# Attention and MLP on one core: the inner layer's upper part in one step for 18 groups, and the first block products' operands in the plan

## The chip, the cores and the metric

The kernel runs on one core of one Trainium2 chip. The metric is the device time of an execution in microseconds (us). Three runs of the kernel before took 776.96, 771.91 and 774.73 us, a median of 774.73; a fourth execution was profiled.

## The reference

Block-sparse attention is followed by a two-layer network (cut; inputs are 4 batches, 8 heads, 768 positions of 64; the network has 3072 tokens, 512 wide, and an inner width of 2048). `w_in` and `w_out` come as 64-bit floats, the rest of the large inputs as 32-bit.

```python
def _attn_ref(q, k, v, sampled_blocks):
    scores = scale * np.matmul(q, k.transpose(0, 1, 3, 2))
    # blocks of 32: neighbours, first and last block, 3 sampled blocks per row
    scores = np.where(mask, scores, -1000000000.0)
    scores = scores - np.max(scores, axis=-1, keepdims=True)
    attn = np.exp(scores)
    attn = attn / (np.sum(attn, axis=-1, keepdims=True) + 1e-09)
    return np.matmul(attn, v).astype(np.float32)

def _moe_ref(x, w_in, w_out, s, b):
    h = x @ w_in
    r = np.maximum(h, 0.0)
    g = s * (r * r) + b
    return (g @ w_out).astype(np.float32)
```

## The kernel before

**Stages.** Attention fills the first 250 us. The network follows in two stages. In the first, tokens 0 to 767 (two groups of 384 tokens) go through the network in 32 *groups*: a group is 384 tokens by 128 of the inner width. In the second, the other 2304 tokens go through it as products of blocks by Strassen's scheme: the inner width is taken in eight passes of two blocks of 128, and each pass needs seven block products instead of eight.

**Accuracy.** A 32-bit product is made of three matmuls. Every operand is split into an upper part (rounded to the type `fp32r` by a copy) and a lower part (operand less upper part): `upper*upper + upper*lower + lower*upper`. So each operand costs a cast on ScalarE (ACT) and a subtraction on VectorE (DVE).

**One group.** `mlp1` makes the first matrix of a group on TensorE (PE), 12 matmuls of 384 columns into bank 0 or 1 by turns (L438 to L440). Then come `relu` (L443, ACT), `square` (L448 on ACT for groups from `SQ` = 24 on, else L450 on DVE, which also multiplies by `s`), `hidden_high` (L454 adds `b`, L455 casts, both on ACT) and `hidden_low` (L459, DVE). `mlp2` makes the second matrix of the group before, nine matmuls of 512 columns (L480 to L482). The tiles are called `hid0` and `hid1` for the working tiles, `hid2` to `hid4` for upper parts and `hid5` to `hid7` for lower ones.

**Weights.** A 64-bit block is loaded by SyncE (SP) into a raw buffer (L62) and decoded into the two parts in nine steps of `decode_f64`: on DVE L85 and L87, L93, L94, L95; on POOL L88; on ACT the sign (L89) and two Relus with a bias (L91, L92). The biases are the tiles `b_top` and `b_most`, filled by POOL at the start. There are 32 blocks, `i0` to `i15` and `o0` to `o15`. Six are decoded during attention, the others beside the groups, and `o15` is the last.

**What sets the order.** An object of class `Plan` collects attention, the decoding and the first `NPL` = 30 groups as operations with an engine, a cost, a priority, dependencies and buffers, and works out an order for every engine; the instructions are then issued in that order, and each engine takes its own strictly one after the other. The costs are written into the code, as in the tuple `cost` of the decoding. Groups 30 and 31 and all block products are issued behind the plan, by loops written out. Which sums and splits stand beside which product is in tables: `EARLY` (behind groups 30 and 31), `FIRST` (behind the products of the first pass), `F_NOW`, `F_NEXT` and so on. A word such as `+S2` is a sum (L575 of weights, L577 and L580 of `x`), `wA21` joins two parts of a weight quarter (L584), `<B11` is a load (SP), `>A21` a store, `hS2` and `lS2` are the upper part (L599, ACT) and the lower part (L601, DVE).

**The first block products.** `product` (L605 to L618) takes two operands, one of weights (A, S) and one of `x` (B, T), and makes six matmuls of 384 columns in bank 0 or 1 by turns (the same two banks as the groups). The order is 1, 2, 6, 7, 5, 3, 4. The plan holds some of the operands already, placed behind the last raw load by `last_load`: loads and splits of B11 and B21, the sums S1, S2, S3, T3, T1, T2, and the two parts of S2. Product 1 is copied by ACT (L1461) and the others are added to it by DVE (L1465 and on). The part before the first product reads:

```python
    EARLY = {30: "hT3 lT3 hS3 lS3", 31: "<B22 hT2 lT2 hT1 hS1"}
    for i in range(NPL, NSUB):
        g, f = subs[i]
        mlp1(i)
        relu(i)
        if i - LAG >= NPL - 1:
            mlp2(i - LAG)
        square(i)
        hidden_high(i)
        hidden_low(i)
        work(0, S0, EARLY.get(i, ""))
```

## Time and profile before

| | |
|---|---|
| median of three runs | 774.73 us |
| profiled execution | 772.34 us |
| its span | 770.6 us |
| mean granted TensorE clock | 0.986 of full speed |
| TensorE busy | 732.4 us |
| DVE busy | 568.1 us |
| ACT busy | 475.1 us |
| POOL busy | 242.1 us |
| moved by DMA | 89.14 MB |

How to read the lines of the profile: a group of instructions is a line of the kernel, engine, operation, tile written and tiles read, partitions by elements, and a count; then the busy time in us, the mean of one in ns, the idle time of the engine just before them and what ended it. A line of the timeline is the start in us from the span's beginning, the duration, the engine, the line, the operation, the tiles, and, in brackets, the idle time ahead and what released it. A line of the stretches is the stretch, its length, the busy time and instruction count of PE, PEld (weight loads of TensorE), DVE, ACT and POOL, the granted clock, the busy share of the DMA engines and GB/s. A line of SP's waits is what the queue waited at and for, then the sum in us, the count and the longest.

### The profile page before, as it was taken

What the parts mean: (1) busy time and instruction counts of PE and PEld (TensorE: products, weight loads), DVE (VectorE), ACT (ScalarE), POOL (GpSimd) and SP (SyncE); (2) the same over time, 40 slices, a digit from 0 to 9 for tenths busy, and PEclk for the clock granted to TensorE, in tenths of its full rate; (3) what the DMA queues carried; (4) which work ended last, traced back from release to release, by engine and by line L of the source; (5) the groups of instructions that cost most, each with busy time, mean ns of one, the idle gap of its engine ahead of it and who ended that gap; (6) DMA issues with size and microseconds to landing.
All of it is one profiled execution on the core that took longest, in us unless ns stands there. A gap on an engine that the chain in (4) does not pass through costs nothing.

```text
span 770.6 us, 21377 instructions
## 1 busy us (share of the span) xinstructions
PE 732.4 (95%) x8032; PEld 619.7 (80%) x8032; DVE 568.1 (74%) x1437; ACT 475.1 (62%) x1143; POOL 242.1 (31%) x398
## 2 busy tenths in 40 slices
PE   8699898999788999999989999999999999999997
PEld 6377675676567999999878998888998998888896
DVE  4767466988586789897896688687678678667652
ACT  3767576888586878789753444565443567344433
POOL 4936244546230221211022232223222232222221
PEclk9989999999899999999999999999999999999999
DMA  8978888877774534635433222224000022000002
GB/s 237 235 199 223 233 215 223 206 202 213 178 202 117 159 110 148 209 118 161 101 126 90 76 83 75 63 69 123 1 1 1 1 62 83 1 1 0 1 1 82
DMA packets 100998, 89.14 MB, mean 116 GB/s; under 512 B 50208, under 2 KB 79520, under 8 KB 100896
## 3 DMA queue, kind: packets, MB, share of 16 engines
q1 hardware_dynamic: 98592, 81.50, 37.8%
q0 software_dynamic: 2304, 6.29, 3.3%
q8 instruction: 63, 1.03, 0.6%
q14 instruction: 39, 0.32, 0.1%
HBM read 68.89 MB, written 14.68 MB: 108 GB/s over the span
## 4 chain that ended last, share of the span: by engine, by line
PE 75%; DVE 9%; ACT 5%; issue 4%; DMA 3%; POOL 1%; SPq 1%; POOLq 0%; ACTq 0%; DVEq 0%
PE m L617 20%; PE o L481 10%; PE o L482 10%; PE o L480 10%; PE xs L1062 5%; PE s L953 5%; PE t L1010 4%; PE h L438 3%; PE h L440 2%; PE h L439 2%; PE od L1052 2%; DVE ptile L970 1%; PE xs L1074 1%; DMA qr_3s<-in_q_dup_dram 1%; DVE xp L601 1%
## 5 line engine op out<-in xcount | busy, mean ns | idle before, releaser
L459 POOL TENSOR_TENSOR hid<-hid,hid 128x384 fp32r<-128x384 f32 x96 | 105.6, 1101 | 292.3 <-ACT hid L635 245.6
L634 ACT ACTIVATE hid<-hid,sb_b,sb_s 128x384 f32<-128x384 f32 x96 | 68.0, 709 | 151.6 <-DVE hid L628 151.5
L982 ACT ACTIVATE ptile<-ptile,nm 128x256 f32<-128x256 f32 (+1 forms) x208 | 107.2, 518 | 35.3 <-DVE nm L970 35.0
L970 DVE CUSTOM_DVE_ANT_1 ptile<-s,mt 128x256 f32<-128x256 f32 x176 | 64.4, 421 | 33.2 <-PE s L953 32.4
L482 PE MATMUL o<-woutr,hid 128*128 128x512 f32 x168 | 66.4, 395 | 0.0
L481 PE MATMUL o<-woutr,hid 128*128 128x512 f32 x168 | 66.3, 395 | 0.0
L480 PE MATMUL o<-woutr,hid 128*128 128x512 f32 x168 | 65.3, 389 | 0.0
L617 PE MATMUL m<-wout,win 128*128 128x384 f32 x264 | 62.6, 340 | 2.1 <-ACT xrest L1461 1.6
L617 PE MATMUL m<-xp,wop 128*128 128x384 f32 x288 | 58.3, 337 | 0.0
L1062 PEld LDWEIGHTS xs<-vA,pt 128*32 128x32 f32 x1696 | 36.6, 113 | 26.9 <-issue 8.5
L481 PE MATMUL o<-win,hid 128*128 128x512 f32 x144 | 56.8, 395 | 0.0
L628 DVE SCALAR_TENSOR_TENSOR hid<-hid 128x384 f32<-128x384 f32 x96 | 54.3, 566 | 3.3
L1010 PE MATMUL t<-ident,ptile 128*128 128x128 f32 x352 | 51.0, 285 | 5.7 <-issue 5.3
L617 PE MATMUL m<-xp,win 128*128 128x384 f32 x288 | 55.1, 338 | 1.4 <-DVE xp L601 0.7
L1062 PE MATMUL xs<-vA,pt 128*32 128x64 f32 x1696 | 49.0, 228 | 6.5 <-issue 5.3
L617 PEld LDWEIGHTS m<-xp,win 128*128 128x128 f32 x288 | 50.9, 188 | 4.5 <-DVE xp L601 1.2
L635 ACT CAST hid<-hid 128x384 fp32r<-128x384 f32 x96 | 49.4, 514 | 7.5 <-PE o L482 0.4
L617 PEld LDWEIGHTS m<-xp,wop 128*128 128x128 f32 x288 | 51.5, 188 | 2.1
L617 PEld LDWEIGHTS m<-wout,win 128*128 128x128 f32 x264 | 47.4, 188 | 5.1 <-ACT xrest L1461 2.5
L482 PE MATMUL o<-win,hid 128*128 128x512 f32 x126 | 49.8, 395 | 0.0
L892 POOL COPY kk<-kt 128x256 f32<-128x256 f32 (+2 forms) x46 | 21.3, 466 | 90.4 <-PE s L953 90.2
L480 PE MATMUL o<-win,hid 128*128 128x512 f32 x126 | 49.2, 391 | 0.2
(191 smaller groups left out, 1860.6 us busy)
## 6 DMA issues: line engine op xcount, KB each, us to landing
vB<-in_v_dram SPq DMA_DIRECT2D x113, 128.0 KB, 4.1
vA<-in_v_dram SPq DMA_DIRECT2D x73, 128.0 KB, 3.9
raw_o<-in_w_out_dram SPq DMA_DIRECT2D x14, 512.0 KB, 3.4
raw_i<-in_w_in_dram SPq DMA_DIRECT2D x12, 512.0 KB, 3.8
xd<-xst SPq DMA_DIRECT2D x44, 128.0 KB, 3.7
out_dram<-ob SPq DMA_DIRECT2D x20, 256.0 KB, 2.0
sum<-xd SPq DMA_DIRECT2D x12, 384.0 KB, 4.2
kt<-in_k_blk_dram SPq DMA_DIRECT2D x8, 384.0 KB, 5.5
```

Source lines behind the costliest of these rows:

```text
L459: (eng or nc.vector).tensor_tensor(out=htile(5 + i % 3), in0=t, in1=gh.bitcast(F32), op=ALU.subtract)
L480: nc.tensor.matmul(acc, gh[:, tsl], wout(f, 0), start=first, stop=False)
L481: nc.tensor.matmul(acc, gh[:, tsl], wout(f, 1), start=False, stop=False)
L482: nc.tensor.matmul(acc, gl[:, tsl], wout(f, 0), start=False, stop=last)
L617: nc.tensor.matmul(to, w_, x_, start=(c == 0 and k == 0), stop=(c == 1 and k == 2))
L628: vec.scalar_tensor_tensor(out=t, in0=t, scalar=0.0, in1=t, op0=ALU.max, op1=ALU.mult)
L634: nc.scalar.activation(t, t, AF.Identity, bias=sb_b, scale=sb_s)
L635: nc.scalar.copy(gh, t)
L970: nc.vector.tensor_tensor_reduce(out=pt, in0=sp, in1=msk, scale=-scale, scalar=FMAX if g == 0 else nm[:, 0:1], op0=ALU.add, op1=ALU.min, a ...
L982: nc.scalar.activation(pt[:, :w], pt[:, :w], AF.Exp, bias=nms[n][:, last:last + 1], scale=-1.0, accum_out=dns[i][:, g, j:j + 1])
L1010: nc.tensor.transpose(tp[:, (2 * j + c) * P:(2 * j + c + 1) * P], src[:, c * P:(c + 1) * P], ident)
L1062: nc.tensor.matmul(xs[quads[pair]], pt[:, c, quads[pair]], vt[:, a, col:col + D], start=(j == 0 and c == 0), stop=(c == 1), tile_position= ...
```

## The change

Four things change.

1. For groups below `SQ` the upper part is made in one step: ACT adds `b` and writes `fp32r` directly, and DVE makes the lower part as (square + `b`) less the upper part, in one operation of three operands. The cast is gone for these groups. For the others the three steps stay.
2. `SQ` goes from 24 to 18, so the squares of groups 18 to 23 are done by ACT.
3. The Relus of the decoding take their biases as numbers in the instruction; the two tiles and their fills on POOL go.
4. The plan's list of operands for the first products grows: the parts of S1, S3, S4 and T2, the joining of A12 and the sums S4 and T4 are added, and the loads and splits of B11 and B21 come first and may be issued from the second matrix of group 18 on, no longer behind the last raw load (the times at which raw blocks are loaded stay as they were). The tables `FIRST` and `EARLY` lose what the plan now holds. The costs that the plan reckons with change as well.

```diff
-    "WARM": 4, "FILL": 4, "FP": -1.0, "NPL": 30, "SQ": 24, "LATE": 3000.0, "M1": 75.6, "M2": 77.7,
+    "WARM": 4, "FILL": 4, "FP": -1.0, "NPL": 30, "SQ": 18, "LATE": 3000.0, "M1": 75.6, "M2": 77.7,
...
-        ("a", lambda: A.activation(mag(F32), mag(), AF.Relu, scale=-8.0, bias=top), (0,)),
-        ("a", lambda: A.activation(mag(), mag(F32), AF.Relu, scale=-1.0, bias=most), (4,)),
+        ("a", lambda: A.activation(mag(F32), mag(), AF.Relu, scale=-8.0, bias=F32_MOST + F64_SHIFT), (0,)),
+        ("a", lambda: A.activation(mag(), mag(F32), AF.Relu, scale=-1.0, bias=F32_MOST), (4,)),
...
     def hidden_high(i):
         t, gh = htile(i % 2), htile(2 + i % 3)
-        nc.scalar.activation(t, t, AF.Identity, bias=sb_b, scale=sb_s if i >= T["SQ"] else 1.0)
-        nc.scalar.copy(gh, t)
+        if i < T["SQ"]:
+            nc.scalar.activation(gh, t, AF.Identity, bias=sb_b)
+        else:
+            nc.scalar.activation(t, t, AF.Identity, bias=sb_b, scale=sb_s)
+            nc.scalar.copy(gh, t)
 
     def hidden_low(i, eng=None):
         t, gh = htile(i % 2), htile(2 + i % 3)
+        if i < T["SQ"]:
+            nc.vector.scalar_tensor_tensor(out=htile(5 + i % 3), in0=t, scalar=sb_b, in1=gh.bitcast(F32), op0=ALU.add, op1=ALU.subtract)
+            return
         (eng or nc.vector).tensor_tensor(out=htile(5 + i % 3), in0=t, in1=gh.bitcast(F32), op=ALU.subtract)
...
-        cost = (400, 420, 800, 670, 720, 720, 550, 390, 690)
+        cost = (420, 470, 950, 670, 630, 630, 700, 480, 760)
...
-            ew[what] = op(eng, cost, N + 600 + len(ew), fn, [*(over if rest else [m2[14], m2[15], last_load]), *(ew[x] for x in deps.split())],
+            ew[what] = op(eng, cost, N + 600 + len(ew), fn, [*(over if rest else [m2[14], m2[15], m2[18]]), *(ew[x] for x in deps.split())],
...
-        for deps, what in (("", "<B11"), ("", "<B21"), ("", "<T1"), ("", "<T3"), ("", "<T2"), ("", "<T4"), ("<B11", "hB11"), ("hB11", "lB11"),
-                           ("<B21", "hB21"), ("hB21", "lB21"), ("", "wA21"), ("", "wA22"), ("wA21 wA22", "+S1"), ("", "wA11"), ("+S1 wA11", "+S2"),
-                           ("+S2", "hS2"), ("<T3 <T1", "+T3"), ("+T3 <T2", "+T1"), ("+T1", "+T2"), ("hS2", "lS2"),
-                           ("+S2", "+S3"), ("+S3", ">A21")):
+        for deps, what in (("", "<B11"), ("", "<B21"), ("<B11", "hB11"), ("hB11", "lB11"), ("<B21", "hB21"), ("hB21", "lB21"),
+                           ("", "<T1"), ("", "<T3"), ("", "<T2"), ("", "<T4"), ("", "wA21"), ("", "wA22"), ("wA21 wA22", "+S1"), ("", "wA11"),
+                           ("+S1 wA11", "+S2"), ("+S2", "hS2"), ("hS2", "lS2"), ("+S2", "+S3"), ("+S3", ">A21"), ("<T3 <T1", "+T3"),
+                           ("+T3 <T2", "+T1"), ("+T1", "+T2"), ("+T2", "hT2"), ("hT2", "lT2"), ("+S3", "hS3"), ("hS3", "lS3"), ("+S1", "hS1"),
+                           ("hS1", "lS1"), ("", "wA12"), ("wA12 +S2", "+S4"), ("+S4", "hS4"), ("hS4", "lS4"), ("+T2 <T4", "+T4")):
...
-    FIRST = {2: "lT1 lS1 wA12 +S4 hS4 hB22", 6: "lS4 +T4 hT4", 7: "lB22", 5: "lT4"}
+    FIRST = {2: "hB22", 6: "hT4", 7: "lB22", 5: "lT4"}
...
-    EARLY = {30: "hT3 lT3 hS3 lS3", 31: "<B22 hT2 lT2 hT1 hS1"}
+    EARLY = {30: "hT3 lT3 hT1", 31: "<B22 lT1"}
```

The order on TensorE is the same in both. ACT's instructions of the kernel before, from the square of group 29 to the upper part of group 30 (`h0_15` is the bank of group 30's first matrix, `wout2` holds B11 and B21, `win2` the parts of S2):

```order
L448 ACTIVATE hid1_5488<-hid1_5488 128x384
L89 ACTIVATE raw_o15_6462<-raw_o15_6462 128x512
L454 ACTIVATE hid1_5488<-hid1_5488,sb_b_63,sb_s_62 128x384
L455 CAST hid4_5522<-hid1_5488 128x384
L91 ACTIVATE wkhp1_430<-wkhp1_430,b_top_64 128x512
L92 ACTIVATE wkhp1_430<-wkhp1_430,b_most_66 128x512
L599 CAST wout2_5734<-wout2_5734 128x12x2x32 x2
L599 CAST win2_6246<-sum2_6572 128x256
L443 ACTIVATE hid0_5464<-h0_15_6594 128x384
L448 ACTIVATE hid0_5464<-hid0_5464 128x384
L454 ACTIVATE hid0_5464<-hid0_5464,sb_b_63,sb_s_62 128x384
```

and those of the kernel after, from the square of group 29 to the Relu of group 30 (`sum3` is S4 and T4, `sum4` A12; `wop` takes the parts of S1 and S3, `win2` those of S2 and S4, `wout2` now the upper part of T2; the lines are the changed kernel's own, L439 is the Relu, L601 an upper part):

```order
L444 ACTIVATE hid1_5483<-hid1_5483 128x384
L91 ACTIVATE wkhp1_426<-wkhp1_426 128x512
L92 ACTIVATE wkhp1_426<-wkhp1_426 128x512
L453 ACTIVATE hid1_5483<-hid1_5483,sb_b_63,sb_s_62 128x384
L454 CAST hid4_5518<-hid1_5483 128x384
L89 ACTIVATE raw_o15_6447<-raw_o15_6447 128x512
L601 CAST wop_6554<-sum0_6549 128x256
L601 CAST win2_6219<-sum2_6551 128x256
L601 CAST wop_6554<-sum1_6550 128x256
L601 CAST win2_6219<-sum3_6552 128x256
L601 CAST wout2_5719<-sum2_6551 128x12x2x32
L439 ACTIVATE hid0_5462<-h0_15_6583 128x384
```

The casts of B11 and B21 have left this place for an earlier one, and the upper parts of S1, S2, S3, S4 and T2 stand ahead of the Relu of group 30, where one of S2 stood.

On DVE, before, from the lower parts of B11 and B21 to the lower part of group 30 (`sum0`, `sum1` and `sum2` are S1, S3 and S2 at 256 columns, and T1, T3 and T2 at 768):

```order
L601 TENSOR_TENSOR wout2_5734<-wout2_5734 128x768 x2
L584 TENSOR_TENSOR whole_6576<-win1_5768 128x256 x2
L575 TENSOR_TENSOR sum0_6570<-whole_6576 128x256
L584 TENSOR_TENSOR whole_6576<-win0_2929 128x256
L575 TENSOR_TENSOR sum2_6572<-sum0_6570,whole_6576 128x256
L575 TENSOR_TENSOR sum1_6571<-whole_6576 128x256
L601 TENSOR_TENSOR win2_6246<-sum2_6572,win2_6246 128x256
L580 TENSOR_TENSOR sum1_6571<-sum1_6571,sum0_6570 128x768
L580 TENSOR_TENSOR sum0_6570<-sum0_6570,sum2_6572 128x768
L580 TENSOR_TENSOR sum2_6572<-sum2_6572,sum1_6571 128x768
L459 TENSOR_TENSOR hid5_5493<-hid0_5464,hid2_5476 128x384
```

and after, from the lower part of S1 to that of group 30; the joining steps and the sums S1, S2 and S3 stand directly ahead of these rows:

```order
L603 TENSOR_TENSOR wop_6554<-sum0_6549,wop_6554 128x256
L603 TENSOR_TENSOR win2_6219<-sum2_6551,win2_6219 128x256
L603 TENSOR_TENSOR wop_6554<-sum1_6550,wop_6554 128x256
L586 TENSOR_TENSOR sum4_6553<-win0_2925 128x256
L577 TENSOR_TENSOR sum3_6552<-sum4_6553,sum2_6551 128x256
L582 TENSOR_TENSOR sum1_6550<-sum1_6550,sum0_6549 128x768
L603 TENSOR_TENSOR win2_6219<-sum3_6552,win2_6219 128x256
L582 TENSOR_TENSOR sum0_6549<-sum0_6549,sum2_6551 128x768
L582 TENSOR_TENSOR sum2_6551<-sum2_6551,sum1_6550 128x768
L579 TENSOR_TENSOR sum3_6552<-sum2_6551,sum3_6552 128x768
L603 TENSOR_TENSOR win2_6219<-sum2_6551,wout2_5719 128x12x2x32
L461 TENSOR_TENSOR hid5_5488<-hid0_5462,hid2_5477 128x384
```

Between S3 and the lower part of group 30 there were the lower part of S2 and three sums of `x`; there are now the lower parts of S1, S2, S3, S4 and T2, the joining of A12, S4, and four sums of `x`.

More of the change, by code (lines that the diff above doesn't have):

```diff
@@ L37, in _i32, with decode_f64 @@
     return x if x < 2 ** 31 else x - 2 ** 32
-def decode_f64(nc, n, src, top, most, raw_of, mag_of, low_of, hi_of, lo_of):
+def decode_f64(nc, n, src, raw_of, mag_of, low_of, hi_of, lo_of):
     box = {}
@@ L260 @@
     sb_b = cpool.tile([P, 1], F32, name="sb_b")
-    b_top = cpool.tile([P, 1], F32, name="b_top")
-    nc.gpsimd.memset(b_top, F32_MOST + F64_SHIFT)
-    b_most = cpool.tile([P, 1], F32, name="b_most")
-    nc.gpsimd.memset(b_most, F32_MOST)
     xd = dpool.tile([B // 2, 2, P, NM, 2, NPAIR, BLK], F32, name="xd")
@@ L384, in decode @@
             src, view = w_out[f * P:(f + 1) * P, :], wout
-        return decode_f64(nc, NW, src, b_top, b_most, *tail, lambda: view(f, 0), lambda: view(f, 1))
+        return decode_f64(nc, NW, src, *tail, lambda: view(f, 0), lambda: view(f, 1))
     xsp, xraw, kg_pairs = {}, {}, {}
@@ L1387 @@
             for c in range(NCC):
-                pm = op("p", 490, N + T["M1"] + k, lambda k=k, c=c: mlp1(k, (c,)), cols=1152, deps=[*ends, xs_ops[(g, c, 1)], wdone[("i", f, 8)], hd.get((k - 2, 0))], order=[pm])
+                pm = op("p", 520, N + T["M1"] + k, lambda k=k, c=c: mlp1(k, (c,)), cols=1152, deps=[*ends, xs_ops[(g, c, 1)], wdone[("i", f, 8)], hd.get((k - 2, 0))], order=[pm])
             dep = pm
-            for m, (eng, c, fn) in enumerate((("a", 480, relu), ("a" if k >= T["SQ"] else "v", 510, square), ("a", 960, hidden_high), ("g" if k < T["LOW"] else "v", 1100 if k < T["LOW"] else 420, hidden_low if k >= T["LOW"] else lambda i: hidden_low(i, nc.gpsimd)))):
+            dv = k < T["SQ"]
+            for m, (eng, c, fn) in enumerate((("a", 480, relu), ("v", 640, square) if dv else ("a", 530, square), ("a", 620 if dv else 1230, hidden_high), ("v", 660 if dv else 560, hidden_low))):
                 dep = hd[(k, m)] = op(eng, c, N - 50 + k, lambda k=k, fn=fn: fn(k), [dep, o_t, hd.get((k - 2, 3)) if m == 0 else None,
@@ L1394 @@
                 g, f = subs[k - 1]
-                pm2 = m2[k - 1] = op("p", 1930, N + T["M2"] + k, lambda k=k: mlp2(k - 1), cols=4608, deps=[*every, hd[(k - 1, 3)], wdone[("o", f, 8)]], order=[pm2])
+                pm2 = m2[k - 1] = op("p", 2090, N + T["M2"] + k, lambda k=k: mlp2(k - 1), cols=4608, deps=[*every, hd[(k - 1, 3)], wdone[("o", f, 8)]], order=[pm2])
         ew = {}
```

2 rows, old and new, of the table T are left out of this document.

## The prediction

> **What bounds the kernel now.** I read the page first, then the busy time in stretches of 15 us, then TensorE's own timeline where those stretches show it idle, and last the two engines that it waits for there.
>
> ```profile
> span 770.6 us, 21377 instructions
> ...
> PE 732.4 (95%) x8032; PEld 619.7 (80%) x8032; DVE 568.1 (74%) x1437; ACT 475.1 (62%) x1143; POOL 242.1 (31%) x398
> ```
>
> TensorE is busy for 95% of the span. From the first inner-layer matmuls (about 250 us) to the end it is short of work in one place only, the passage from the planned inner layer to the first block products:
>
> ```profile
> 345.00:360.00 15.00, 15.00 (x76) 13.47 (x75) 11.45 (x19) 13.86 (x25) 3.69 (x4) 1.00 0.32 107
> 360.00:375.00 15.00, 15.00 (x77) 13.51 (x76) 12.41 (x24) 10.95 (x19) 0.91 (x1) 1.00 0.78 186
> 375.00:390.00 15.00, 13.65 (x65) 11.25 (x63) 13.50 (x24) 12.34 (x24) 0.65 (x1) 1.00 0.36 112
> 390.00:405.00 15.00, 12.83 (x60) 10.62 (x61) 14.62 (x29) 7.95 (x16) 5.42 (x5) 1.00 0.34 112
> ```
>
> The columns are busy time and instruction count of PE, PEld, DVE, ACT and POOL, then the granted clock. 76 or 77 matmuls fit in a full stretch; the two behind it hold 65 and 60, and TensorE lacks 1.35 and 2.17 us, 3.5 us in all. This is the pool that the moved operands can save, and since the end of a matmul is modelled and hides a little of each gap, starts say more than idle times:
>
> ```profile
> 376.02 0.39 PE L480 MATMUL o<-woutr,hid 128*128 128x512 f32 x1
> 378.10 1.22 PE L617 MATMUL m<-wout,win 128*128 128x384 f32 x6
> 379.81 1.32 PE L617 MATMUL m<-wout,win 128*128 128x384 f32 x6 [0.49 <-ACT hid L443]
> 380.97 0.39 PE L480 MATMUL o<-win,hid 128*128 128x512 f32 x1
> 383.80 0.44 PE L617 MATMUL m<-wout,win 128*128 128x384 f32 x1 [0.59 <-ACT xrest L1461]
> 389.32 0.41 PE L617 MATMUL m<-xp,win 128*128 128x384 f32 x1
> 390.09 1.14 PE L617 MATMUL m<-xp,win 128*128 128x384 f32 x5 [0.36 <-DVE xp L601]
> ```
>
> At 376.02 stands the second matrix of group 29, at 378.10 and 379.81 products 1 and 2, at 380.97 the second matrix of group 30, at 383.80 product 6, at 389.32 product 3. Six matmuls of 384 columns need 1.05 us when nothing waits and nine of 512 need 2.08 (376.02 to 378.10). So product 2 came 0.66 late, product 6 came 0.75 late, and product 3 lost 0.6 between its first matmul and the rest. Product 2 waits for ACT's Relu of group 31 (it needs that bank), product 6 for the copy that empties bank 0, product 3 for the low part of B22. What feeds these is one chain through DVE and ACT. The timeline of DVE (start, length, line, tiles written and read):
>
> ```profile
> 370.04 0.69 DVE L93 TENSOR_TENSOR win<-wkhp,raw_o 128x512 fp32r<-128x512 f32 x1 [0.82 <-ACT wkhp L92]
> ...
> 371.90 1.82 DVE L601 TENSOR_TENSOR wout<-wout 128x768 fp32r<-128x768 f32 x2
> 373.64 0.76 DVE L584 TENSOR_TENSOR whole<-win 128x256 f32<-128x256 f32 x2
> ...
> 375.57 0.42 DVE L575 TENSOR_TENSOR sum<-whole 128x256 f32<-128x256 f32 x1
> ...
> 376.47 2.93 DVE L580 TENSOR_TENSOR sum<-sum,sum 128x768 f32<-128x768 f32 x3
> ```
>
> and that of ACT, from the Relu of group 29 on:
>
> ```profile
> 365.87 0.49 ACT L443 ACTIVATE hid<-h 128x384 f32<-128x384 f32 x1
> ...
> 368.53 0.72 ACT L91 ACTIVATE wkhp<-wkhp,b_top 128x512 f32<-128x512 int32 x1
> 369.28 0.72 ACT L92 ACTIVATE wkhp<-wkhp,b_most 128x512 int32<-128x512 f32 x1
> ...
> 375.69 0.41 ACT L599 CAST win<-sum 128x256 fp32r<-128x256 f32 x1 [4.22 <-DVE sum L575]
> 376.00 0.49 ACT L443 ACTIVATE hid<-h 128x384 f32<-128x384 f32 x1
> 376.52 0.53 ACT L448 ACTIVATE hid<-hid 128x384 f32<-128x384 f32 x1
> 377.08 0.71 ACT L454 ACTIVATE hid<-hid,sb_b,sb_s 128x384 f32<-128x384 f32 x1
> 377.81 0.51 ACT L455 CAST hid<-hid 128x384 fp32r<-128x384 f32 x1
> 378.23 0.83 ACT L599 CAST xp<-sum 128x768 fp32r<-128x768 f32 x1
> 378.97 0.40 ACT L599 CAST wop<-sum 128x256 fp32r<-128x256 f32 x1
> ```
>
> 365.87 is the Relu of group 29, and it stands right behind that group's first matrix on TensorE, so nothing in this change brings it forward. 370.04 begins the last steps of the last weight block (o15). 375.69 is the cast of S2, for which ACT idled 4.22 us; the Relu of group 30 (376.00) was queued behind it and late by that. An engine takes its instructions in order: what stands ahead of a Relu here is added to it.
>
> **The change, part by part.** The sum is against the profiled execution, 772.34 us (span 770.6 and 1.7 around it). That one lies 2.4 under the median of the three runs, 774.73; the four together have a mean of 774.0, and the forecast is made from that.
>
> *One step for the upper part, six squares moved.*
>
> ```profile
> L459 DVE TENSOR_TENSOR hid<-hid,hid 128x384 fp32r<-128x384 f32 x32 | 18.8, 587 | 8.5 <-ACT hid L455 8.5
> L450 DVE SCALAR_TENSOR_TENSOR hid<-hid,sb_s 128x384 f32<-128x384 f32 x24 | 14.9, 622 | 4.1 <-ACT hid L443 3.9
> L455 ACT CAST hid<-hid 128x384 fp32r<-128x384 f32 x32 | 16.5, 514 | 1.3
> L454 ACT ACTIVATE hid<-hid,sb_b 128x384 f32<-128x384 f32 x24 | 14.6, 610 | 3.5 <-DVE hid L450 3.4
> L89 ACT ACTIVATE raw_o<-raw_o 128x512 f32<-128x512 f32 x16 | 10.8, 674 | 0.3 <-issue 0.3
> ```
>
> 18 casts of 514 ns leave ACT (-9.3 us) and six squares of 0.53 (the row at 376.52) come to it (+3.2). On DVE six squares of 622 leave (-3.7); 18 lower parts become a form with one more operand that the trace has only as the square, so each goes from 587 to somewhere between the same 587 and 622, at most +0.6 in all, which I take. The Relus of the decoding lose their bias operand: between nothing and the 0.08 by which the 610 of an activation with one operand exceeds the 0.53 of one without, 52 times in this stretch, up to -4.2. All of that lies beside a TensorE that is full (77 matmuls) and runs three groups ahead of the lower parts, so I cost it at nothing; that cover would be gone if ACT needed more than TensorE's 4.1 us a group (77 matmuls in 15 us, 21 a group), which is a rival below.
>
> *Planner's costs, order in attention.* TensorE's order does not change by a row. On DVE, ACT and POOL the decoding steps of the first six blocks move by at most eight maxima. Their sum stays, DVE has idle time between, and I see no sign for it: 0, with 3 us either way as the bound. The two bias fills that POOL loses stand ahead of everything, under the first loads: 0.
>
> *Loads of B11 and B21.* SP issues them ahead of the last five raw blocks.
>
> ```profile
> SPq L62 <- DVE win L93: 30.6, 9, 5.4
> ```
>
> The raw loads behind them wait anyway for a buffer that DVE must free, nine times 3.4 us on average, so two issues hide in that. Without this cover it would be about a microsecond on one block.
>
> *The operands.* DVE: the lower parts of B11 and B21 (371.90 to 373.64) now come earlier, so the first of the sums follows the last block directly. Is the last block earlier? ACT has, from the Relu of group 29 on and each from its start to the next one's, that Relu and the square (0.52 + 0.56), the two Relus of o15 (0.75 + 0.63), scale and bias and the cast (0.73 + 0.42), 3.6 in all, and only then o15's sign (0.67): 365.87 + 4.3 = 370.1, against 370.04 before. Not earlier. The first sum then starts at 371.9 in place of 373.64.
>
> From there before: 1.93 to S3 (375.57). Now the lower parts of S1, S2 and S3, the joining of A12 and S4 stand between S3 and T3: six steps of 0.34 and 0.1 for a cast, 2.1. Then T3, T1 and T2 (2.93, the row at 376.47) with the lower part of S4 among them (0.34). T2 is ready at 371.9 + 1.93 + 2.1 + 3.27 = 379.2. ACT's order now has the upper parts of S1, S2, S3, S4 and T2 all ahead of the Relu of group 30. So it starts 0.05 and one wide cast (0.74, 378.23 to 378.97) later, at 380.0, and ends 0.5 later, 380.5. Product 1 needs that bank, and it started at 378.10: **a new wait of 2.4 us**. Behind its start come the four steps of that group (2.2) and two wide casts for T3 and T1 (1.48): the Relu of group 31 starts at 383.7 and ends at 384.2. Product 2 starts there in place of 379.81: 4.4 later.
>
> Group 30's second matrix follows 1.16 behind (380.97 - 379.81) and takes 2.08, so product 6 starts at 387.4 and finds bank 0 empty (383.7, four steps 2.2, the copy some 0.5 as the cast at 377.81: 386.4): 3.6 later than 383.80, its 0.75 of waiting is gone. Product 3 finds B22 split, which takes off another 0.6 to 0.8: 2.9. Product 4 waits, as before, for T4's lower part behind product 5's sums, and the sums for the second pair run behind that on DVE as before. From 405 us on TensorE is full in both. The waits add **+2.9**.
>
> *The clock.* Two waits with one short product between them are a case of their own:
>
> ```profile
> 76.73:80.14 3.41, 1.45 (x51) 1.36 (x52) 0.61 (x3) 1.60 (x8) 1.17 (x4) 1.00 1.08 274
> 80.14:83.55 3.41, 3.41 (x55) 1.85 (x56) 1.25 (x4) 0.86 (x2) 0.19 (x1) 0.50 1.05 238
> ...
> 199.61:203.02 3.41, 1.64 (x13) 1.16 (x21) 1.25 (x3) 0.28 (x2) 0.94 (x1) 0.50 0.77 215
> 203.02:206.43 3.41, 3.41 (x98) 2.18 (x82) 1.47 (x8) 2.47 (x8) 1.43 (x4) 0.50 0.17 52
> ...
> 390.75:394.16 3.41, 2.35 (x11) 1.72 (x10) 3.40 (x5) 1.83 (x4) 1.34 (x2) 1.00 0.64 231
> ```
>
> TensorE's clock changes in steps of 3.41 us. A step with 1.45 us of matmuls is followed by one at 0.50, one at half clock with 1.64 by another at 0.50; one with 2.35 is followed by full clock (the stretch from 390 shows 1.00). Between 378.1 and 384.2 there will be one product, some 1.2 us of matmuls in 6.1. Wherever the steps fall, one of them holds less than 1.45, and the step behind it reaches 0.8 to 1.7 us, counted as loss, into products that nothing else delays: **+1.3**. The Trainium skill (TensorE: Matmul & The Clock Gate, Part 1 and "HAM oscillation") gives the window as 3413 ns, free-running, and sums its rule up as no idle gaps above about 3.4 us. By that sentence gaps of 2.4 and 2.6 would cost nothing, and the sum would be +2.9 alone; the trace's rows, where 1.45 us of work in a window did not hold the clock, speak against it.
>
> Sum: 2.9 + 1.3 = +4.2. On the profiled execution 776.5, on the mean of the four 778.2.
>
> **The rivals.**
>
> (a) *The same waits, the clock held.* The steps of 3.41 us fall so that each holds more than 1.64 of matmuls, or the gate asks for longer gaps than these: +2.9, 776.9. Against it stand the rows at 76.73 and 199.61. (The sentence of the Trainium skill above would come out here too.)
>
> (b) *The operands are in time.* If DVE and ACT reached o15's end some 5 us sooner, the casts would be done when group 30's Relu is due, and the late starts named (0.66, 0.75, 0.6) and the later ones go, all told 3.5 by the idle time and some 5.5 by starts: 768.5 to 770.5. For it: both engines lose work. Against: the Relu of group 29 waits for TensorE, and every step behind it is in a row on one queue.
>
> (c) *ACT becomes the bound* in groups 18 to 29, slower. A group there costs ACT its four steps (2.2), and a block with it 0.75 + 0.63 + 0.67: 4.3 with the old bias operand, 4.1 without, against TensorE's 4.1. For it stands the stretch from 345, where four such groups (24 to 27) begin and ACT is busy for 13.86 of 15 us. If DVE's mask comes 0.5 late for each, 12 groups lose about 6 us, and o15 and with it product 1 come later by as much: 784. It decides as soon as a group takes ACT over 4.2. Against it: in the same stretch TensorE has its 76 matmuls, and the next one leaves ACT 4 us.
>
> (d) *Attention's fetch stall.* One long wait there is for nothing the profile shows:
>
> ```profile
> 196.78 4.59 issue
> ```
>
> It falls where the DMA engines are full, and two steps at half clock follow. If the loads that move by one place there spare it, 4.6 and some 2.5 for the clock go: 778.2 - 7.1 = 771. Nothing says that they do.
>
> **How the numbers follow.** Forecast 0.37, 774 to 783 with attention's 3; (a) 0.20; (b) 0.17; (c) 0.15; (d) 0.11. The likeliest is 778.2. The range leaves out a part of (b) that attention's 3 takes lower and the upper half of (c): 768 to 784. A measurement of this kernel tells about 1% from no change, so faster is under 767, slower over 782.5. Faster: a quarter of (b) and as much of (d), should attention's 3 come on top, 0.08 with what I have not thought of. Slower: two thirds of (c) and a tenth of the forecast, 0.14. Within 1%: 0.78.
>
> **What would show it.** Right: product 1 with a wait of 2 to 3 us on ACT's Relu, product 2 with another, both Relus behind a cast that waits for DVE's T2; the sums starting near 371.9; a step at 0.50 near 382 to 388; no wait at product 6 nor for B22; 76 or 77 matmuls a stretch up to there. Wrong: the sums beginning before 368 (b), ACT's Relus behind their matmuls by more than a microsecond from group 18 (c), another length of attention, seen in when group 0 starts, by more than 3 us (d).

## The result, and the profile after

The changed kernel takes 782.87 us in the median of four executions (780.44 to 785.73); the kernel before takes 773.94, the three runs above and one of 773.15. The ratio is 1.0119, with a 95% interval of 1.0085 to 1.0154: slower by 9 us, where the forecast was 4 us slower (778.2, range 768 to 784). The profiled execution took 783.09 us, its span is 781.3. Ratios, here and below, leave disturbed executions out, so they need not be the ratio of the medians.

By the starts of TensorE's matmuls in the two profiles, the span divides like this:

| | before | after | difference |
|---|---|---|---|
| start of the span to the first matmul of group 0 (attention) | 246.61 | 252.45 | +5.84 |
| group 0 to group 18 | 70.90 | 71.71 | +0.81 |
| group 18 to group 31 | 56.43 | 56.43 | 0.00 |
| group 31 to the first product of the second pass (the junction) | 21.83 | 25.81 | +3.98 |
| from there to the last matmul of a block product | 361.21 | 361.20 | -0.01 |

The junction came out as forecast. What the forecast had set to nothing is attention. The 0.81 between groups 0 and 18 had no term either; the kernels below spread from 70.75 to 71.68 there, so no cause is given for it.

**The junction.** The stretches of the kernel after, in the same columns as before:

```profile
360.00:375.00 15.00, 15.00 (x75) 13.39 (x74) 11.14 (x20) 13.74 (x26) 1.77 (x2) 1.00 0.34 100
375.00:390.00 15.00, 12.01 (x56) 10.13 (x54) 12.30 (x23) 7.28 (x14) 0.00 (x0) 0.91 0.52 113
390.00:405.00 15.00, 13.29 (x57) 11.70 (x58) 9.84 (x15) 9.79 (x18) 2.19 (x2) 0.87 0.35 121
```

The full stretches up to 375 hold 75 to 79 matmuls; the next two hold 56 and 57 (65 and 60 before), and the granted clock is 0.91 and 0.87, where it was 1.00. TensorE's timeline:

```profile
386.90 2.10 PE L619 MATMUL m<-wout,win 128*128 128x384 f32 x6 [1.99 <-ACT hid L439]
390.60 2.29 PE L619 MATMUL m<-wout,win 128*128 128x384 f32 x6 [1.59 <-ACT hid L439]
392.68 0.63 PE L482 MATMUL o<-win,hid 128*128 128x512 f32 x1
...
395.35 0.33 PE L619 MATMUL m<-wout,win 128*128 128x384 f32 x1
...
400.60 1.22 PE L619 MATMUL m<-xp,win 128*128 128x384 f32 x6
```

Product 1 (386.90) and product 2 (390.60) wait for ACT's Relu (L439 here), 2.16 and 1.94 us by starts, and take 2.10 and 2.29 us (1.22 and 1.32 before). Product 6 (395.35) and product 3 (400.60, all six in a row) wait for nothing. DVE's and ACT's timelines show what the Relu stands behind:

```profile
377.77 0.69 DVE L95 SCALAR_TENSOR_TENSOR win<-wklp,wkhp 128x512 fp32r<-128x512 int32 x1
378.38 0.75 DVE L586 TENSOR_TENSOR whole<-win 128x256 f32<-128x256 f32 x2
...
380.31 0.42 DVE L577 TENSOR_TENSOR sum<-whole 128x256 f32<-128x256 f32 x1
...
383.65 1.95 DVE L582 TENSOR_TENSOR sum<-sum,sum 128x768 f32<-128x768 f32 x2
```

```profile
382.56 0.41 ACT L601 CAST win<-sum 128x256 fp32r<-128x256 f32 x1 [1.39 <-DVE sum L577]
385.63 0.83 ACT L601 CAST wout<-sum 128x768 fp32r<-128x768 f32 x1 [2.66 <-DVE sum L582]
386.37 0.48 ACT L439 ACTIVATE hid<-h 128x384 f32<-128x384 f32 x1
...
388.60 1.56 ACT L601 CAST xp<-sum 128x768 fp32r<-128x768 f32 x2
390.06 0.48 ACT L439 ACTIVATE hid<-h 128x384 f32<-128x384 f32 x1
```

The last step of the last weight block is at 377.77, the joining begins at 378.38, T2 is the second of the two sums at 383.65 and ends at 385.6. Its upper part (385.63) is the cast that ACT waited 2.66 us for, and the Relu of group 30 (386.37) is behind it; that of group 31 (390.06) is behind the casts of T3 and T1.

**Attention.** Of TensorE's waits, summed by what ended them, this one grew most there; the columns are the sum, the count and the longest. Before and after:

```profile
PE xs L1074 <- DVE xss L1068: 3.3, 3, 1.8
```

```profile
PE xs L1076 <- DVE xss L1070: 6.9, 4, 2.1
```

`xss` is the attention output times the reciprocal of its sum, which TensorE transposes. The same wait at another tile (`od`) fell from 2.3 to 0.6, so all waits for `xss` together grew by 1.9. Two of the places, on TensorE:

```profile
157.60 0.44 PE L1076 MATMUL xs<-ident,xss 128*128 128x128 f32 x2 [1.79 <-DVE xss L1070]
...
187.54 0.44 PE L1076 MATMUL xs<-ident,xss 128*128 128x128 f32 x2 [1.56 <-DVE xss L1070]
```

In the kernel before the same two transposes start 0.11 and 0.40 us behind the matmul ahead of them. DVE around the first of them, before and then after:

```profile
147.27 0.69 DVE L95 SCALAR_TENSOR_TENSOR win<-wklp,wkhp 128x512 fp32r<-128x512 int32 x1
...
151.29 0.42 DVE L970 CUSTOM_DVE_ANT_1 ptile<-s,mt 128x256 f32<-128x256 f32 x1
...
152.12 0.42 DVE L1068 TENSOR_TENSOR xss<-xs,rc 128x256 f32<-128x256 f32 x1
152.46 1.27 DVE L1021 COPY dp<-t 96x512 f32<-96x512 f32 x2
```

```profile
153.72 0.42 DVE L972 CUSTOM_DVE_ANT_1 ptile<-s,mt 128x256 f32<-128x256 f32 x1
154.06 1.53 DVE L95 SCALAR_TENSOR_TENSOR win<-wklp,wkhp 128x512 fp32r<-128x512 int32 x1
155.52 1.27 DVE L1023 COPY dp<-t 96x512 f32<-96x512 f32 x2
...
157.12 0.42 DVE L1070 TENSOR_TENSOR xss<-xs,rc 128x256 f32<-128x256 f32 x1
```

L95 is the last decoding step of a weight block, and L1023 copies two transposed tiles. Before, the multiplication starts 0.83 us after the last maximum; the decoding step had been done at 147.27, ahead of the maxima. After, the decoding step and the two copies stand between, it is 3.40 us, and TensorE waits 1.79 of them. At the second place two decoding steps (L94 and L95) stand between in both kernels. After, a third step (L93) and a copy have joined them:

```profile
184.19 0.69 DVE L93 TENSOR_TENSOR win<-wkhp,raw_i 128x512 fp32r<-128x512 f32 x1
...
186.06 0.68 DVE L1023 COPY pt<-t 128x512 f32<-128x512 f32 x1
...
187.06 0.42 DVE L1070 TENSOR_TENSOR xss<-xs,rc 128x256 f32<-128x256 f32 x1
```

From the last maximum to the multiplication it is 2.03 us before and 3.21 after.

### The profile page after: what moved, and what is told of

Read it like the earlier page. It is cut to its first block, busy times and chain, and to the rows that moved or that the text cites. A ratio compares the mean times of both kernels' runs of the same rounds, so it can differ in the third digit from the quotient of the medians.

```text
span 781.3 us, 21363 instructions
## 1 busy us (share of the span) xinstructions
PE 733.1 (94%) x8032; PEld 623.2 (80%) x8032; DVE 568.0 (73%) x1431; ACT 466.6 (60%) x1131; POOL 241.1 (31%) x396
## 4 chain that ended last, share of the span: by engine, by line
PE 79%; DVE 9%; issue 4%; DMA 3%; ACT 3%; SPq 1%; ACTq 0%; DVEq 0%
PE m L619 20%; PE o L483 10%; PE o L484 10%; PE o L482 10%; PE s L955 6%; PE t L1012 5%; PE xs L1064 5%; PE h L434 3%; PE h L436 3%; PE h L435 3%; PE od L1054 2%; DVE ptile L972 2%; DMA vB<-in_v_dram 2%; PE xs L1076 1%; PE s L933 1%
## 5 line engine op out<-in xcount | busy, mean ns | idle before, releaser
L619 PE MATMUL m<-wout,win 128*128 128x384 f32 x264 | 64.3, 348 | 4.6 <-ACT hid L439 3.6
L483 PE MATMUL o<-win,hid 128*128 128x512 f32 x144 | 57.0, 396 | 0.0
L1064 PE MATMUL xs<-vA,pt 128*32 128x64 f32 x1696 | 47.0, 224 | 7.2 <-issue 6.2
L484 PE MATMUL o<-win,hid 128*128 128x512 f32 x126 | 50.0, 397 | 0.0
L905 POOL COPY kk<-kt 128x256 f32 x132 | 49.8, 416 | 0.0
```

Source lines behind the costliest of these rows:

```text
L483: nc.tensor.matmul(acc, gh[:, tsl], wout(f, 1), start=False, stop=False)
L484: nc.tensor.matmul(acc, gl[:, tsl], wout(f, 0), start=False, stop=last)
L619: nc.tensor.matmul(to, w_, x_, start=(c == 0 and k == 0), stop=(c == 1 and k == 2))
L905: nc.gpsimd.tensor_copy(flat(kg[:, a:a + 1]), flat(kts[e][:, bass.ds(j, 1)]))
L1064: nc.tensor.matmul(xs[quads[pair]], pt[:, c, quads[pair]], vt[:, a, col:col + D], start=(j == 0 and c == 0), stop=(c == 1), tile_position= ...
```

## The experiments

There are two theories. *Junction:* a Relu that TensorE needs stands in ACT's queue behind casts of sums that DVE makes late. *Attention:* the new costs of the decoding steps put a step on DVE ahead of work that TensorE waits for. Against the second stands that attention's length varies by itself. The experiments were run on three further occasions, each beside the kernel before, whose median was 772.54 beside 1 to 4, 772.42 beside 5 to 8 and 771.60 beside 9 to 12. Two numbers are read from the one profile of every kernel: the start of group 0, and the *stretch*, from the first matmul of group 18 to the first product of the second pass. 8 and 10 were executed once, so their profiles are compared and not their times.

| kernel | median, us | ratio to before (95%) | group 0 starts | stretch |
|---|---|---|---|---|
| before | 773.94 | | 246.61 | 78.26 |
| after | 782.87 | 1.0119 (1.0085 to 1.0154) | 252.45 | 82.24 |
| 1 old decoding costs | 778.03 | 1.0082 (1.0050 to 1.0115) | 246.24 | 83.48 |
| 2 old list | 773.93 | 1.0036 (1.0011 to 1.0061) | 249.50 | 76.43 |
| 3 before, new decoding costs | 776.95 | 1.0063 (1.0041 to 1.0085) | 249.92 | 78.98 |
| 4 before, new list | 781.46 | 1.0121 (1.0089 to 1.0154) | 250.82 | 85.27 |
| 5 old list and costs | 771.93 | 1.0008 (0.9979 to 1.0037) | 244.58 | 77.39 |
| 6 Relus ahead of T's casts | 776.05 | 1.0051 (1.0020 to 1.0082) | 248.86 | 76.62 |
| 7 the same, old costs | 777.06 | 1.0043 (1.0010 to 1.0075) | 245.06 | 81.07 |
| 8 group 31 made twice | 784.40 (one) | | 254.68 | 82.27 |
| 9 Relus first, old costs | 769.76 | 0.9979 (0.9953 to 1.0005) | 245.37 | 76.34 |
| 10 both gaps filled | 778.08 (one) | | 248.70 | 81.02 |
| 11 before, new costs on DVE | 779.53 | 1.0110 (1.0075 to 1.0144) | 247.61 | 82.19 |
| 12 before, new costs on ACT | 770.61 | 0.9972 (0.9947 to 0.9998) | 246.78 | 76.41 |

### 1 to 4: one part undone, one part alone

**1.** The changed kernel with the old costs of the decoding steps:

```diff
-        cost = (420, 470, 950, 670, 630, 630, 700, 480, 760)
+        cost = (400, 420, 800, 670, 720, 720, 550, 390, 690)
```

> The changed kernel, but the plan reckons with the old costs of the nine decoding steps; nothing else is touched. The order of attention on every engine is then that of the kernel before, but for one decoding step; the Relu of group 30 still stands behind the cast of T2. Theory A (the new costs move the decoding steps in attention, and that costs the 5 to 6 us by which group 0 starts later): group 0 starts near 247 instead of 252.45, the junction still loses 4, and the time is near 778. Rival B (attention's length differs by chance from one execution to the next, whatever the order): the time stays near 783, and over several kernels the start of group 0 does not follow the order. Rival C (one step for the upper part or the missing bias tiles slow attention): 783.

Group 0 starts at 246.24 and the time is 778.03: theory A's numbers. The junction keeps its loss, and 1.2 us more (stretch 83.48).

**2.** The changed kernel with the list of operands and the tables of the kernel before:

```diff
-            ew[what] = op(eng, cost, N + 600 + len(ew), fn, [*(over if rest else [m2[14], m2[15], m2[18]]), *(ew[x] for x in deps.split())],
+            ew[what] = op(eng, cost, N + 600 + len(ew), fn, [*(over if rest else [m2[14], m2[15], last_load]), *(ew[x] for x in deps.split())],
...
-    FIRST = {2: "hB22", 6: "hT4", 7: "lB22", 5: "lT4"}
+    FIRST = {2: "lT1 lS1 wA12 +S4 hS4 hB22", 6: "lS4 +T4 hT4", 7: "lB22", 5: "lT4"}
...
-    EARLY = {30: "hT3 lT3 hT1", 31: "<B22 lT1"}
+    EARLY = {30: "hT3 lT3 hS3 lS3", 31: "<B22 hT2 lT2 hT1 hS1"}
```

> The changed kernel with the old list of operands in the plan, the old tables behind groups 30 and 31 and behind the first products, and the loads of B11 and B21 behind the last raw load again. Attention's order is that of the changed kernel. Theory (the longer list puts the Relu of group 30 behind the cast of T2, 4 us with the clock): time near 779, product 1 starts without a wait, no stretch at half clock there, and group 0 starts near 252 as in the changed kernel. Rival (the list costs nothing net, the loss is the one-step form's or ACT's load): time stays near 783.

The time fell further than expected, to 773.93. The stretch (76.43) is not only 4 but 5.8 us shorter than in the changed kernel, and 1.8 shorter than in the kernel before; and group 0 starts at 249.50, not near 252. The stretch in which that one had 65 matmuls is full here:

```profile
375.00:390.00 15.00, 15.00 (x79) 13.82 (x78) 11.48 (x20) 11.09 (x22) 0.00 (x0) 1.00 0.31 98
```

Group 0 is late against the kernel before by 2.9, half of what the changed kernel's profile shows.

**3.** The kernel before with the new costs of the decoding steps, and nothing else (the first diff the other way round).

> The kernel before with only the new costs of the nine decoding steps in the plan. Not one instruction is other, only their order. Theory A: group 0 starts 4 to 6 us later than in the kernel before (246.6), near 252, and the time is near 779. Rivals B and C: same as before, 774.

776.95, a ratio of 1.0063 with an interval of 1.0041 to 1.0085: 3 to 7 us for eight numbers that change no instruction. Group 0 starts 3.3 later, a little less than the 4 to 6 expected, and the stretch is 0.7 longer.

**4.** The kernel before with the new list alone (the second diff the other way round, and the list).

> The kernel before with only the new list of operands in the plan, its tables, and the earlier loads of B11 and B21; attention's order is that of the kernel before. Theory (queued Relu, and clock): product 1 waits some 2 us for the Relu of group 30, product 2 again, both run at half clock, the time is 4 us over before, near 778. Rival (the waits arise only together with the earlier decoding of the changed kernel): within 1 us of before.

Product 2 waits 2.5 us and ends at half clock. Product 1 waits only 0.3 and runs at full clock, since TensorE reaches it late: the time is 9 us over before, not 4, because TensorE waits in another place, for the parts of a weight block (`woutr`) in the second matrix of group 28:

```profile
375.82 0.50 PE L480 MATMUL o<-woutr,hid 128*128 128x512 f32 x1 [1.86 <-DVE woutr L93]
377.08 0.50 PE L481 MATMUL o<-woutr,hid 128*128 128x512 f32 x1 [0.76 <-DVE woutr L95]
```

Two waits of 1.86 and 0.76, and matmuls at a lower clock behind them, make group 18 to group 31 4.7 us longer. The changed kernel has no such wait (56.43, as before), nor has 1, with the same list and the same decoding costs, so it shows only together with the rest of the kernel before. That it comes from the parts of B11 and B21 (0.82 us each on ACT, 1.81 together on DVE), which stand among the last decoding steps here, is argued from the order and not shown; 11 below speaks against it, for it has the same wait with the old list. Group 0 started at 250.82 here though attention's order is the old one: attention does vary by itself.

### 5 to 7, and 9: what is left, and the Relus moved ahead

**5.** Old list and old decoding costs, both diffs in one.

> The changed kernel with both the old list of operands and the old decoding costs: what is left of the change is the one-step upper part, six squares more on ACT, the biases as numbers and the other costs of the plan. Measured by the stretch from the first matmul of group 18 to the first product of the second pass, the kernel before takes 78.26 us, the changed one 82.24, the one with the old list 76.43. Theory (the losses are the list's and the decoding costs', the rest gains by itself because the parts of B11 and B21 and the last block are done earlier): the stretch near 76.5, group 0 near 247, time 1 to 3 us under before, 770 to 772. Rival (with the old costs the last block is late again): stretch 78, time as before. Rival (attention's length is chance): group 0 near 250, time 773 to 775.

Group 0 at 244.58, stretch 77.39, ratio 1.0008 (0.9979 to 1.0037): the expected gain of 1 to 3 us is not there. Beside the old list and costs, the rest of the change (one step for the upper part, six squares, biases as numbers, the plan's other costs) is worth nothing that can be measured. Beside the new list it may be worth something: 4, without it, has the wait for a weight block that 1, with it, has not.

**6.** The changed kernel with the parts of the T operands behind the Relus:

```diff
-                           ("+T3 <T2", "+T1"), ("+T1", "+T2"), ("+T2", "hT2"), ("hT2", "lT2"), ("+S3", "hS3"), ("hS3", "lS3"), ("+S1", "hS1"),
+                           ("+T3 <T2", "+T1"), ("+T1", "+T2"), ("+S3", "hS3"), ("hS3", "lS3"), ("+S1", "hS1"),
...
-    FIRST = {2: "hB22", 6: "hT4", 7: "lB22", 5: "lT4"}
+    FIRST = {2: "hT1 lT1 hB22", 6: "hT4", 7: "lB22", 5: "lT4"}
...
-    EARLY = {30: "hT3 lT3 hT1", 31: "<B22 lT1"}
+    EARLY = {30: "", 31: "<B22 hT2 lT2 hT3 lT3"}
```

> The changed kernel with the parts of T2 taken out of the plan and issued behind group 31, those of T3 behind them and those of T1 behind product 2, so that the Relus of groups 30 and 31 stand ahead of the casts of all T. Theory (queue order at ACT is the whole of the junction's loss): product 1 starts right behind the second matrix of group 29, the stretch from group 18 to the second pass falls from 82.24 to 76 to 78, half clock is gone, time near 777 to 778 (attention still late). Rival (T2 is simply late on DVE, and the wait only moves from products 1 and 2 to product 6): stretch 79 to 81.

No work was removed, and the stretch is 76.62 against 82.24. Product 1 and product 2 have no wait, and the clock stays at full speed. The whole loss of the junction, and 1.6 us more, was the order in which the parts of T stand to the two Relus. The casts on ACT are what the Relus stood behind; the lower parts on DVE moved along with them.

**7.** The same edit with the old decoding costs.

> As the kernel before this one in the list, and with the old decoding costs. If both theories hold (queue order at the junction, decoding costs in attention), it is faster than the kernel before by 1 to 3 us: stretch 76 to 78, group 0 near 247, 770 to 772. If attention's length is chance or the list of the changed kernel costs in the groups too: 774 to 778.

The expectation missed: 777.06, with group 0 early (245.06) and the stretch at 81.07. With the other costs the plan puts the sum S4 behind the three T sums on DVE, and the cast of S4 is still ahead of the Relu of group 30. ACT, then TensorE:

```profile
378.70 0.40 ACT L601 CAST win<-sum 128x256 fp32r<-128x256 f32 x1 [4.12 <-DVE sum L577]
379.02 0.48 ACT L439 ACTIVATE hid<-h 128x384 f32<-128x384 f32 x1
```

```profile
379.55 1.32 PE L619 MATMUL m<-wout,win 128*128 128x384 f32 x6 [2.25 <-ACT hid L439]
```

4.12 us of waiting for S4, the Relu directly behind, and product 1 waits 2.25 for it: the same fault with another operand.

**9.** So the parts of S4 go behind the Relus too:

```diff
-                           ("hS1", "lS1"), ("", "wA12"), ("wA12 +S2", "+S4"), ("+S4", "hS4"), ("hS4", "lS4"), ("+T2 <T4", "+T4")):
+                           ("hS1", "lS1"), ("", "wA12"), ("wA12 +S2", "+S4"), ("+T2 <T4", "+T4")):
...
-    FIRST = {2: "hT1 lT1 hB22", 6: "hT4", 7: "lB22", 5: "lT4"}
+    FIRST = {2: "hT1 lT1 hS4 hB22", 6: "lS4 hT4", 7: "lB22", 5: "lT4"}
```

> The changed kernel with the old decoding costs, and with the parts of S4, T2, T3 and T1 all behind the Relus of groups 30 and 31 (those of S4 and T1 behind product 2). In the run that kept the parts of S4 in the plan, ACT waited 4.12 us for the sum S4 ahead of the Relu of group 30, and product 1 waited 2.25 us for that Relu. Theory (whatever cast stands ahead of the Relu is added to it): product 1 has no wait, the stretch from group 18 to the second pass is 75.5 to 77.5 (81.07 there), with group 0 near 246.5 the time is 769 to 771, 1.5 to 3 us under before. Rival (the sums on DVE are late anyway, and the lower part of group 30 or of T2 makes the next wait): stretch 78 to 80, time as before.

The stretch is 76.34 and the time 769.76; by the ratios (0.9979 and 1.0119) that is about 11 us under the changed kernel. Against the kernel before the ratio is 0.9979 with 1.0005 at its upper end, so a gain over it is likely and not shown.

### 8 and 10: what the clock costs

**8.** The changed kernel with the first matrix of group 31 made twice. Its second making overwrites the first, so it only fills TensorE's first gap:

```diff
         mlp1(i)
+        if i == NSUB - 1:
+            mlp1(i)
         relu(i)
```

> The changed kernel, with the first matrix of group 31 made twice (the second time overwrites the first): 12 matmuls, 2.08 us, that fill the place where product 1 waits and change nothing else that it waits for. The forecast's step on the clock (a window of 3.41 us with less than 1.45 us of matmuls sends the next to half clock): products 1 and 2, which take 2.10 and 2.08 us to their next in the changed kernel, run at full clock (1.05 each) or one of them does, and the stretch from group 18 to the second pass falls by 0.8 to 1.7 us from 82.24. Rival (gaps of 2 us do not touch the clock, the slow products wait for something else): stretch the same, 82.2, or longer by what the extra matmuls push back.

The expectation missed: 82.27. Product 1 ran at full clock, but the half clock moved one gap further, behind the start of product 2. Windows of 3.41 us, cut where the clock steps (the granted clock is the figure behind POOL's):

```profile
389.37:392.78 3.41, 1.23 (x7) 0.93 (x6) 1.51 (x2) 3.31 (x7) 0.00 (x0) 1.00 0.17 51
392.78:396.19 3.41, 3.41 (x10) 2.77 (x9) 2.46 (x4) 1.97 (x5) 0.00 (x0) 0.50 0.00 0
```

**10.** As 8, with product 1 made three times:

```diff
                 to = product(p, s, n)
+                if s == S0 and p == 0 and n == 1:
+                    for _ in range(2):
+                        turns[0] -= 1
+                        to = product(p, s, n)
```

> The changed kernel with the first matrix of group 31 made twice, as in the run before, and product 1 made three times: 12 more matmuls, 2.1 us, into the gap between products 1 and 2, which was 2.35 us there with the next 4 us at half clock. Theory (a window of 3.41 us short of matmuls sends the next to half clock, one gap of 2.35 us is enough): no stretch at half clock from product 1 on, product 2 starts when it did (it waits for the Relu of group 31), and the stretch from group 18 to the second pass falls from 82.27 to 80.3 to 81.3. Rival (the clock falls there for another reason than missing matmuls): half clock again, 82.3 or more.

24 more matmuls than the changed kernel, and the stretch is 81.02. The clock stays at full speed:

```profile
375.00:390.00 15.00, 14.83 (x77) 13.16 (x76) 11.37 (x22) 9.23 (x18) 0.00 (x0) 1.00 0.45 97
```

In 8, product 2 waits for the Relu of group 31. In 10 it starts 0.4 later, behind the added matmuls, and the stretch is 1.25 shorter all the same. From product 2's first matmul to the second pass 8 takes 15.85 us and 10 takes 14.18. So the half clock costs 1.25 to 1.67 us at the junction, in these two profiles.

### 11 and 12: which engine's order, in attention

**11.** The kernel before with the new costs for DVE's five decoding steps:

```diff
-        cost = (400, 420, 800, 670, 720, 720, 550, 390, 690)
+        cost = (420, 470, 800, 670, 720, 720, 700, 480, 760)
```

> The kernel before with the new costs for DVE's decoding steps alone. The last decoding step of a block then stands ahead of the multiplication of the attention output (xss) in the places where the changed kernel has it; SP's order stays almost as before (6 rows of difference, 26 with all the new costs). In the traces so far all five kernels with the new costs have TensorE wait for xss near 157 and 187 us (1.7 to 1.8 and 1.1 to 1.7 us), none of the five with the old costs does. Theory (DVE's queue order is the cause): both waits are there, group 0 starts 3 us later than the 246.7 that the five kernels with the old costs have in the mean, time 3 to 5 us over before. Rival (SP's stores standing behind the raw loads are the cause): as before.

Both waits for `xss` are there:

```profile
154.07 0.44 PE L1074 MATMUL xs<-ident,xss 128*128 128x128 f32 x2 [1.64 <-DVE xss L1068]
...
182.88 0.44 PE L1074 MATMUL xs<-ident,xss 128*128 128x128 f32 x2 [1.41 <-DVE xss L1068]
```

Group 0 starts only 0.9 later than the mean of the old order, not 3. The time is 8 us over before all the same: in the profile 5.8 are lost between groups 18 and 31 (62.19), to waits for a weight block as in 4 (1.98 and 0.56 us, and half clock), and 1.8 are won at the junction. So the waits for `xss` follow DVE's order, and most of this kernel's loss is another one.

**12.** The kernel before with the new costs for ACT's steps:

```diff
-        cost = (400, 420, 800, 670, 720, 720, 550, 390, 690)
+        cost = (400, 420, 800, 670, 630, 630, 550, 390, 690)
```

> The kernel before with the new costs for ACT's three decoding steps alone. SP's order is then changed in 28 rows, near to the changed kernel's, while on DVE the last decoding step of each block stays on the other side of xss, as before. Theory (DVE's queue order is the cause): no wait for xss near 157 and 187 us, group 0 near 247, time within 1.5 us of before. Rival (SP's stores): group 0 3 us later, time 3 to 5 us over before.

Group 0 at 246.78 and no time lost, though SP's order is changed in 28 rows: the rival about the stores falls. The stretch is 76.41, as short as in 2, 6 and 9, from two changed costs alone; the time is 770.61, ratio 0.9972 (0.9947 to 0.9998), the lowest ratio measured here and barely clear of 1. ACT's timeline has where the 1.8 us come from:

```profile
364.58 0.72 ACT L91 ACTIVATE wkhp<-wkhp,b_top 128x512 f32<-128x512 int32 x1
365.33 0.72 ACT L92 ACTIVATE wkhp<-wkhp,b_most 128x512 int32<-128x512 f32 x1
366.12 0.49 ACT L443 ACTIVATE hid<-h 128x384 f32<-128x384 f32 x1
...
373.87 0.41 ACT L599 CAST win<-sum 128x256 fp32r<-128x256 f32 x1 [3.53 <-DVE sum L575]
```

The two Relus of the last weight block now run ahead of the Relu of group 29 (366.12), where they ran 2.7 and 3.4 us behind it. The block and the sums are ready sooner, the cast of S2 ends at 374.3, just as the first matrix of group 30 does, and neither product 1 nor product 2 waits.

**The fourteen profiles together.** In all seven with the new order of DVE (after, 2, 3, 6, 8, 10, 11) the two transposes near 157 and 187 us start 1.9 to 2.1 and 1.4 to 2.0 us behind the matmul ahead of them. In the seven with the old order it is 0.11 in every one at the first place and 0.11 to 0.72 at the second. From a matmul shortly ahead of these places to one shortly behind (at 135.97 and 189.98 in the kernel before) the seven new ones take 58.2 us in the mean, the old ones 54.7: 3.4 us. The two waits are up to 3.3 of it, a third one (last section) up to 1.5, and some is made up in between. In three of the seven (after, 2, 8) the clock falls too: the 3.41 us around the first wait hold 1.62 or 1.63 us of matmuls, and the next 3.41 run at 0.50, which none of the old order does there. Group 0 starts at 250.2 in the mean against 246.5, with a standard deviation of 2.5 and 2.1 from profile to profile, so the 3.7 between the means is three times its standard error of 1.2, while a single profile can say little.

## Why the prediction was right, and where it was not

With the 6.65 us subtracted by which the changed kernel reaches group 30 later, its steps stand against the forecast like this:

| step of the forecast | forecast | measured |
|---|---|---|
| joining and sums begin | 371.9 | 371.7 |
| T2 ready | 379.2 | 378.9 |
| Relu of group 30 starts | 380.0 | 379.7 |
| new wait of product 1 | 2.4 | 2.16 |
| Relu of group 31 starts | 383.7 | 383.4 |
| product 2 later by | 4.4 | 4.14 |
| product 6 starts, with the clock's 1.3 | 388.7 | 388.7 |
| junction, waits and clock | +4.2 | +3.98 |

**The junction** holds step by step, and 6 shows the cause by putting the casts of T behind the Relus. No wait at product 6 nor for B22: right.

**The clock** was right in size (+1.3; 8 and 10 give 1.25 to 1.67). That leaves 2.3 to 2.7 of the 3.98 for the waits, which were forecast at 2.9. The changed kernel's own windows:

```profile
383.74:387.15 3.41, 1.42 (x7) 0.85 (x6) 3.34 (x4) 1.49 (x3) 0.00 (x0) 1.00 0.51 115
387.15:390.56 3.41, 1.86 (x6) 1.34 (x5) 1.82 (x3) 3.33 (x6) 0.00 (x0) 0.50 0.11 38
390.56:393.98 3.42, 3.38 (x10) 3.10 (x11) 1.57 (x3) 2.12 (x4) 0.00 (x0) 0.50 0.02 5
```

1.42 us of matmuls, and the next two windows are at 0.50. One thing in that step was wrong: it called two waits with a short product between them a case of their own. In 8 a single gap of 2.35 us did it, with 1.23 us of matmuls in its window. The Trainium skill (TensorE: Matmul & The Clock Gate, "HAM oscillation") sums its rule up as no idle gaps above about 3.4 us; with a gap of 2.35 us the trace does not agree.

**Attention** is the step that failed: "Their sum stays, DVE has idle time between, and I see no sign for it: 0, with 3 us either way as the bound." The sum of the work did stay, 568.1 and 568.0 us on DVE. But DVE, with its idle time, still ran these rows in order, and a decoding step and a copy or two issued between the last maximum and the multiplication delay the one thing there that TensorE is waiting for. Two such places cost up to 3.3 us. The prediction had used just this rule at the junction and did not apply it to the rows that moved in attention. The rest of the 5.84 is not shown to be the order's: 2.84 is a wait near 139 us whose cause stays open (last section), and equal orders differ by as much (246.61 in the kernel before, 250.82 in 4). One of the forecast's own signs of being wrong did come, another length of attention by more than 3 us. The forecast had tied it to (d), the long wait, and that one stayed.

**The upper part in one step, the squares, the biases** at nothing: right (5), beside the old list. The terms were near, each a little past its bound: the Relus of the decoding lost 0.09 each (624 ns for 716, forecast 0 to 0.08), and the lower part with one more operand costs 635 ns for 587 (forecast up to 622):

```profile
L91 ACT ACTIVATE wkhp<-wkhp 128x512 f32<-128x512 int32 x32 | 20.0, 624 | 1.2 <-DVE wkhp L85 1.1
...
L459 DVE SCALAR_TENSOR_TENSOR hid<-hid,sb_b,hid 128x384 fp32r<-128x384 f32 x18 | 11.4, 635 | 2.8 <-ACT hid L451 2.8
```

The 1.8 us by which the junction could be shorter with all that (2, 6, 9) had no term, and 12 has it without any of these edits. The forecast had written that every step behind the Relu of group 29 is in a row on one queue; in 12 two of those steps went ahead of that Relu.

**The rivals.** (a), the clock held: no. (b), operands in time: no, the sums began at 371.7 and not before 368. (c), ACT as the bound from group 18: no, groups 18 to 31 take 56.43 in both kernels. (d), the long wait in attention: it stayed (4.43 after, 4.59 before).

The range held the time (782.87 under 784), and that is partly luck: its upper end came from half of (c), which did not happen, and attention moved by 5.84, outside the 3 us that had been set as its bound. "Slower by over 1%" had been given 0.14, and it came about by the forecast's junction and by attention.

## What to carry to other kernels

Where engines take their work in order, look at every moved row for what stands behind it: a step put ahead of a Relu, a multiplication or a cast that the bound engine waits for can cost its own length and whatever it waits for, however idle its engine is on average. A planner's costs move such rows without changing one instruction: two numbers gave a ratio of 0.9972 here and five gave 1.0110, while the edits of the changed kernel without its list and decoding costs gave 1.0008. Issue what frees the bound engine's buffers first, and the operands of work that comes later behind it.
